# Three pads in SBUF that shift the operand tiles of a long-convolution and MLP kernel

## The chip, the cores and the metric

The kernel runs on one core of a Trainium2 chip. The metric is the device time of one execution in microseconds (us). Three runs of the kernel before are given by their median.

## The reference

Two kinds of layer follow one another twice on a sequence of 2048 tokens with 1024 channels, all in float32. Layer A normalises x, makes a short causal convolution of k (4 taps) times v, convolves that along the sequence with a long filter per channel (through a Fourier transform in the reference), and gates it with the normalised x. Layer B is an MLP with 3584 hidden units and a squared ReLU.

```python
def _A_ref(q, k, v, shift_k, ssm_k, ssm_D):
    ...
    kv = k_shift * v
    ...
    y = y + kv * ssm_D[None, None, :]
    return q * y

def _B_ref(x, w1, b1, w2, b2):
    h = jnp.einsum("bsd,df->bsf", x, w1) + b1
    zero = jnp.zeros_like(h)
    r = jnp.where(h > zero, h, zero)
    h = r * r
    out = jnp.einsum("bsf,fd->bsd", h, w2) + b2
    return out

x = A_q
x = x + _A_ref(_layernorm(x, axis=-1), A_k, A_v, A_shift_k, A_ssm_k, A_ssm_D)
x = x + _B_ref(_layernorm(x, axis=-1), B_w1, B_b1, B_w2, B_b2)
x = x + _A_ref(_layernorm(x, axis=-1), A_k, A_v, A_shift_k, A_ssm_k, A_ssm_D)
x = x + _B_ref(_layernorm(x, axis=-1), B_w1, B_b1, B_w2, B_b2)
```

## The kernel before

The sequence is cut into four blocks of 512 tokens. The long convolution does not depend on the layer's x, so it is made once for each block, and both passes use it. Eight units of MLP work (two passes by four blocks, in the order of ORDER at the top of the file) run one after another on TensorE. The pieces of the convolution of later blocks are slipped between their matmuls by generators (fwd_x and fwd_g from line 352, prod_stream from line 518), paced by a hand-made rate per unit. The first block has a small planner of its own (Plan, first_block, line 1052), which puts its operations in order by estimated costs.

Precision: each float32 operand is split in a high part, rounded to the fast float32 format of TensorE, and a low part, the rest. mm3 (line 333) makes one product as three matmuls, each 128 x 128 stationary by 512 (or 256) moving columns: high by high (line 334), high by low (335), low by high (336). All times of the MLP on TensorE stand on these three lines.

A unit is a list of steps. One step takes one weight tile of 128 x 512 in two parts, whl, and makes 12 matmuls with it:

- "m1" (line 1795): the first product. The stationary operand is a 128-column piece of whl, the moving operand is xh or xl, the two parts of the normalised x of the block, transposed, 8 tiles of 512 columns each.
- "m2" (line 1842): the second product. The stationary operand is a 128-column piece of rh or rl, the two parts of the squared ReLU of the hidden units, and the moving operand is one half of whl (512 columns).
- "w2" (line 1825), in the last three units (WINO): the second product in a scheme with seven products for eight. The stationary operand is a piece of rh and rl, or of sums of these, which relu_w (line 1540) puts into buffers of the convolution that are free by then: high parts in cx and cg, low parts in cp and fy. The moving operand is again a half of whl.

A weight tile comes to whl in one of two ways: as a raw tile wr that ScalarE rounds (line 1006) and VectorE or GpSimd subtracts (line 1014), or, from its second use on, as a stored pair in one load (line 1004). Loads go through SyncE's queue. The matmuls of the convolution on lines 334 to 336 have the constant tables fh, fl, ih, il as stationary operand and fx, fg, yh or yl as moving operand, 256 columns wide. Those of the first block (line 1089) are unsplit float32.

SBUF is given out by pools, one behind another in each partition: const, cv, pre, mw, and then ml. Before ml exists, the pool pro of the first block uses the same place. Inside a pool, the tiles follow one another in the order of their first making. Each is rounded up to a multiple of 32 bytes, and a name with n buffers takes n such places. Every tile starts at the same address in all 128 partitions. All large tiles but fx are multiples of 512 bytes long, so a pool's small tiles and its start decide where the large ones stand modulo 512. In the kernel before this gives:

| tiles | pool | bytes above a multiple of 512 |
|---|---|---|
| ident, fh, fl, ih, il | const | 128 |
| fx (4 buffers of 2080) | cv | 352, 384, 416, 448 |
| yh, yl, fg, cx, cg, cp, fk, sm, fy | cv | 480 |
| px | pre | 448 |
| xh, xl, wr, whl | mw | 384 |
| rh, rl, acc, yt | ml | 0 |

The tile b1t, the biases of the hidden units, is 28 columns of float32 (112 bytes, 128 with rounding) and stands first in ml, ahead of rh. It is loaded once (line 1480) and read by ScalarE (lines 1486 and 1546).

Of the kernel before, what the change touches and what calls it, by code (L numbers as in the profile page):

```python
# [10 lines left out]
F32 = mybir.dt.float32  # L11
# [8 lines left out]
P = 128  # L20
# [4 lines left out]
FT = F // P  # L25
# [22 lines left out]
PACE_SLACK = {1: 74, 3: 10}  # L48
PACE_TO = {1: 2}
PLAIN = 1  # L50
FILL = (16, 45, 8)
WINO = (5, 6, 7)
WMAKE = 4
# [186 lines left out]
def tile_h3_mlp(ctx: ExitStack, tc: tile.TileContext, q, kT, vT, shk, ssmT, ssmD, w1, b1, w2, b2,  # L240
                fwd_t, pro_t, inv_t, sgn_t, out):
    nc = tc.nc
    V, A, G, PE, SY = nc.vector, nc.scalar, nc.gpsimd, nc.tensor, nc.sync
# [3 lines left out]
    const = ctx.enter_context(tc.tile_pool(name="const", bufs=1))  # L247
    cv = ctx.enter_context(tc.tile_pool(name="cv", bufs=1))
    pre = ctx.enter_context(tc.tile_pool(name="pre", bufs=1))
# [13 lines left out]
    def fill(o, n):  # L263
        for _ in range(n):
            PE.transpose(o[:, 0:P], ident, ident)

    def mkfx(shape, dt=F32):
        return cv.tile(shape, dt, name="fx", bufs=4)

    def mkfg(shape, dt=F32):  # L270
        return cv.tile(shape, dt, name="fg", bufs=3)
# [12 lines left out]
    def const_split():  # L284
        if not halved:
            halved.append(True)
            split(plain[0][:, 0:4], fh, fl)
            split(plain[0][:, 4:6], ih, il)
# [5 lines left out]
    epst = const.tile([P, 1], F32)  # L294
    V.memset(epst, EPS)
    warm = const.tile([P, 1], F32)
    A.activation(warm, epst, AF.Copy)

    def tokens(t, b, tt):
# [52 lines left out]
    def fwd_x(sb, c):  # L352
# [18 lines left out]
        yield  # L371
        if sb <= PLAIN:
            xt = mkfx([P, T])
# [11 lines left out]
        for e in range(2):  # L385
            for r in range(2):
                q_ = slice(e * 256, e * 256 + 256)
                ou = oa[e][:, r * 256:r * 256 + 256]
                if sb <= PLAIN:
                    PE.matmul(ou, plain[0][:, 2 * e + r], xt[:, q_], start=True, stop=True)  # L390
# [37 lines left out]
    def fwd_g(sb, c):  # L428
# [7 lines left out]
        for _ in range(FWD_WAIT):  # L436
            yield
        if sb > PLAIN:
            hi = mkfg([P, T], F32R)
# [8 lines left out]
        for r in range(2):  # L448
            ob = oa[r].rearrange("p (b e c) -> p e b c", b=BT, e=2)
            for e in range(2):  # L450
                q_ = slice(e * 256, e * 256 + 256)
                if sb <= PLAIN:
                    PE.matmul(ob[:, e], plain[0][:, 2 * e + r], raw[:, q_], start=True, stop=True)
# [24 lines left out]
        for i in (1, 2, 0):  # L478
# [5 lines left out]
            yield  # L484
        if sb <= PLAIN:
            yield
# [12 lines left out]
    def fwd_stream(kind, fwd):  # L499
        for sb in range(1, NB):  # L500
            if sb > PLAIN:
                const_split()
# [506 lines left out]
    def w_lo():  # L1009
        n = ptr["lo"]  # L1010
        t = wts[n] = his.pop(n)
        if not from_pair(n):
            e = WLO.get(phase[0], "V")
            ENG[e[n % len(e)]].tensor_sub(t[:, 1], raws[n]["t"], t[:, 0].bitcast(F32))  # L1014
            drop(raws.pop(n))
        ptr["lo"] += 1
# [7 lines left out]
    def w_advance(s, w):  # L1024
# [17 lines left out]
        while ptr["lo"] <= w:  # L1042
# [3 lines left out]
                w_hi()  # L1046
            w_lo()

    mw = ctx.enter_context(tc.tile_pool(name="mw", bufs=1))
    rs = {}  # L1050

    def first_block():
# [27 lines left out]
        with tc.tile_pool(name="pro", bufs=1) as pro:  # L1080
# [119 lines left out]
            def carry_part(c, rows, cols):  # L1200
# [3 lines left out]
                def mmk(e):  # L1204
                    if c == KT - 1:
                        fill(o.t, FILL[0])
                    for r in range(2):
# [175 lines left out]
            def tail(t):  # L1383
                x = x1[t]
                norm(ns[t], x, [(x, h) for h in range(KT)], tails[t // 2], t % 2, NORM_0)
                for kh in range(2):
# [3 lines left out]
                    def tr(e, kh=kh, o=o, idle=idle):  # L1390
# [3 lines left out]
                        for x in idle:  # L1394
                            fill(x.t, FILL[2])
                    pl.add([("PE", 600)], tr, [(ns[t], kh)], [o, *idle])
# [79 lines left out]
    xT = first_block()  # L1476
    pds = prod_stream()
    ml = ctx.enter_context(tc.tile_pool(name="ml", bufs=1, reuse_waits="tile"))
    b1t = ml.tile([P, FT], F32, name="b1t", bufs=1)
    SY.dma_start(b1t, b1)  # L1480
    lag = slag

    def relu2(st, k):
# [139 lines left out]
    def chain(accs, b, xh, xl, ready):  # L1623
# [36 lines left out]
        def stage(st, k):  # L1660
# [31 lines left out]
            elif k in (7, 8):  # L1692
                n = k - 7
                for kh in range(2):
                    o = ps1()
                    if tts[n] == 2 and kh == 0:
                        fill(o, FILL[1])
                    for c in range(4):
# [267 lines left out]
```

## Time and profile before

| what | value |
|---|---|
| runs of the kernel before | 2758.86, 2754.60, 2755.72 us |
| median | 2755.72 us |
| the profiled execution, from its first to its last instruction | 2756.1 us |
| mean granted TensorE clock | 0.992 |
| matmuls, as many weight loads | 12601 |
| data moved by DMA | 756.88 MB, 275 GB/s in the mean |

The profiled execution is as long as its span of 2756.1 us; nothing around it is listed apart. PE is TensorE's matmuls, PEld its weight loads, DVE VectorE, ACT ScalarE, POOL GpSimd, SP SyncE. In a group line, `out<-in` are the names of the tiles written and read, `x` the count, then busy time in us, mean of one in ns, and the idle time of the engine just before, with what ended it. Matmuls overlap one another: the time from one start to the next start is shorter than the duration of one. In a line of the timeline the first number is the start in us, the second the duration. In a line of the view by windows there follow, behind the window and its length, the busy time and count of each engine (all of them, or the chosen one), the granted clock, the DMA share and GB/s. In a line of the waits: who waited for whom, us in total, times, and the longest.

### The profile page before, as it was taken

What the parts mean: (1) busy time and instruction counts of PE and PEld (TensorE: products, weight loads), DVE (VectorE), ACT (ScalarE), POOL (GpSimd) and SP (SyncE); (2) the same over time, 40 slices, a digit from 0 to 9 for tenths busy, and PEclk for the clock granted to TensorE, in tenths of its full rate; (3) what the DMA queues carried; (4) which work ended last, traced back from release to release, by engine and by line L of the source; (5) the groups of instructions that cost most, each with busy time, mean ns of one, the idle gap of its engine ahead of it and who ended that gap; (6) DMA issues with size and microseconds to landing.
All of it is one profiled execution on the core that took longest, in us unless ns stands there. A gap on an engine that the chain in (4) does not pass through costs nothing.

```text
span 2756.1 us, 36563 instructions
## 1 busy us (share of the span) xinstructions
PE 2694.2 (98%) x12601; PEld 2237.7 (81%) x12601; DVE 1935.9 (70%) x3068; ACT 1110.9 (40%) x1937; POOL 826.3 (30%) x531
## 2 busy tenths in 40 slices
PE   7999899899999999999999999999999999999999
PEld 7888787887788888888788888888788788888887
DVE  7878797677787677778676655376787666664555
ACT  4354344433434333342233422244355454444443
POOL 2345564244542645326454265000100010001000
PEclk9999999999999999999999999999999999999999
DMA  8889898589988898788887877688898766676555
GB/s 260 267 298 321 281 311 287 199 302 351 305 294 308 305 330 294 272 303 302 317 286 259 310 270 286 217 290 292 303 308 274 289 229 214 226 275 204 176 164 202
DMA packets 378057, 756.88 MB, mean 275 GB/s; under 512 B 43904, under 2 KB 159248, under 8 KB 377872
## 3 DMA queue, kind: packets, MB, share of 16 engines
q1 hardware_dynamic: 377872, 754.55, 79.8%
q8 instruction: 99, 1.62, 0.2%
q14 instruction: 86, 0.70, 0.1%
HBM read 604.46 MB, written 149.95 MB: 274 GB/s over the span
## 4 chain that ended last, share of the span: by engine, by line
PE 86%; DVE 6%; DMA 5%; issue 1%; ACT 1%; SPq 1%; POOL 0%; DVEq 0%; ACTq 0%; POOLq 0%
PE p L334 26%; PE p L335 26%; PE p L336 26%; PE p L1089 2%; DMA wr<-w 1%; PE pt L336 1%; PE pt L335 1%; PE pt L334 1%; DVE whl L1014 1%; DMA whl<-wd_m 1%; DMA wd_m<-whl 0%; PE pt L594 0%; PE p L788 0%; DVE sm L528 0%; DMA cg<-gd 0%
## 5 line engine op out<-in xcount | busy, mean ns | idle before, releaser
L334 PE MATMUL p<-xh,whl 128*128 128x512 f32 (+1 forms) x1840 | 710.3, 386 | 20.2 <-DVE rl L1492 19.0
L524 POOL TENSOR_TENSOR cp<-cx,cg 128x384 f32<-128x384 f32 (+5 forms) x288 | 534.0, 1867 | 617.7 <-DVE sm L528 397.7
L336 PE MATMUL p<-xh,whl 128*128 128x512 f32 (+1 forms) x1840 | 705.9, 384 | 0.0
L335 PE MATMUL p<-xl,whl 128*128 128x512 f32 (+1 forms) x1840 | 705.5, 383 | 0.1
L1006 ACT CAST whl<-wr 128x512 fp32r<-128x512 f32 x638 | 385.9, 622 | 450.1 <-PE p L336 274.8
L334 PE MATMUL p<-whl,rh 128*128 128x512 f32 x1372 | 547.8, 399 | 1.8 <-DMA whl<-wd_m 1.7
L335 PE MATMUL p<-whl,rh 128*128 128x512 f32 x1372 | 543.0, 396 | 4.9 <-DVE whl L1014 4.9
L1014 DVE TENSOR_TENSOR whl<-wr,whl 128x512 fp32r<-128x512 f32 x624 | 489.4, 805 | 76.9 <-ACT whl L1006 72.1
L336 PE MATMUL p<-whl,rl 128*128 128x512 f32 x1372 | 542.3, 395 | 0.0
L334 PEld LDWEIGHTS p<-xh,whl 128*128 128x128 f32 x1840 | 347.7, 189 | 91.0 <-DVE rl L1492 11.9
L336 PEld LDWEIGHTS p<-xh,whl 128*128 128x128 f32 x1840 | 347.4, 189 | 68.2
L335 PEld LDWEIGHTS p<-xl,whl 128*128 128x128 f32 x1840 | 347.6, 189 | 66.5 <-DVE xl L1402 0.3
L335 PEld LDWEIGHTS p<-whl,rh 128*128 128x128 f32 x1372 | 259.4, 189 | 64.0 <-DVE whl L1014 6.4
L334 PEld LDWEIGHTS p<-whl,rh 128*128 128x128 f32 x1372 | 259.2, 189 | 62.2 <-DMA whl<-wd_m 4.0
L336 PEld LDWEIGHTS p<-whl,rl 128*128 128x128 f32 x1372 | 259.0, 189 | 60.7
L528 DVE TENSOR_REDUCE sm<-cp 128x128 f32<-128x384 f32 (+5 forms) x288 | 249.8, 875 | 13.2 <-POOL cp L524 11.4
L1590 POOL TENSOR_TENSOR acc<-acc,px 128x512 f32<-128x512 f32 x18 | 23.1, 1318 | 770.3 <-DMA px<-b 770.3
L1486 ACT ACTIVATE p<-p,b1t 128x512 f32<-128x512 f32 x138 | 91.7, 664 | 395.6 <-PE p L336 395.4
L1492 DVE TENSOR_TENSOR rl<-p,rh 128x512 fp32r<-128x512 f32 x138 | 94.9, 688 | 221.0 <-ACT rh L1489 220.8
L1554 DVE TENSOR_TENSOR rl<-wr,rh 128x256 fp32r<-128x256 f32 x84 | 51.0, 607 | 207.6 <-ACT rh L1549 207.4
L1613 DVE TENSOR_TENSOR acc<-p,acc 128x512 f32<-128x512 f32 x152 | 101.5, 688 | 90.8 <-PE p L336 90.3
L1546 ACT ACTIVATE wr<-p,b1t 128x512 f32<-128x512 f32 x84 | 58.0, 690 | 188.5 <-PE p L336 184.9
(280 smaller groups left out, 3306.0 us busy)
## 6 DMA issues: line engine op xcount, KB each, us to landing
whl<-wd_m SPq DMA_DIRECT2D x382, 512.0 KB, 5.1
wr<-w SPq DMA_DIRECT2D x494, 256.0 KB, 5.3
wr<-td SPq DMA_DIRECT2D x152, 256.0 KB, 4.2
wd_m<-whl SPq DMA_DIRECT2D x70, 512.0 KB, 6.2
cx<-xd SPq DMA_DIRECT2D x48, 512.0 KB, 5.4
cg<-gd SPq DMA_DIRECT2D x48, 512.0 KB, 6.5
gd<-fg SPq DMA_DIRECT2D x72, 256.0 KB, 6.7
cx<-xd SPq DMA_DIRECT2D x48, 384.0 KB, 6.1
```

Source lines behind the costliest of these rows:

```text
L334: PE.matmul(o, lh, rh, start=start, stop=False)
L335: PE.matmul(o, lh, rl, start=False, stop=False)
L336: PE.matmul(o, ll, rh, start=False, stop=stop)
L524: G.tensor_mul(pr.rearrange("p c i -> p i c"), xt[:, 0:j + 1], gt[:, j::-1])
L528: V.tensor_reduce(sm[:, ty, jj], st["pr"], axis=AX.X, op=OP.add)
L1006: A.copy(t[:, 0], raws[n]["t"])
L1014: ENG[e[n % len(e)]].tensor_sub(t[:, 1], raws[n]["t"], t[:, 0].bitcast(F32))
L1089: PE.matmul(o, lh, r, start=start, stop=stop)
L1486: A.activation(o, o, AF.Relu, bias=b1t[:, st["f"]:st["f"] + 1])
L1492: V.tensor_sub(st["lo"], o, st["hi"].bitcast(F32))
L1546: A.activation(r, st["o"], AF.Relu, bias=b1t[:, st["f"]:st["f"] + 1])
L1613: V.tensor_add(accs[tt][:, d], o, accs[tt][:, d])
```

## The change

Two tiles that nobody reads are added, and one tile is widened.

- pad_c, 104 columns of float32 (416 bytes), at the end of the pool const. It moves everything behind it.
- pad_p, 24 columns (96 bytes), the first tile of the pool pre. Each of the two pads is set to 0 once by VectorE.
- b1t, from 28 to 128 columns (512 bytes), the first tile of the pool ml. Its load writes the first 28 columns as before.

```diff
+PAD_C, PAD_P = 104, 24
...
     warm = const.tile([P, 1], F32)
+    pad_c = const.tile([P, PAD_C], F32)
+    V.memset(pad_c, 0.0)
     A.activation(warm, epst, AF.Copy)
...
+    pad_p = pre.tile([P, PAD_P], F32)
+    V.memset(pad_p, 0.0)
     mw = ctx.enter_context(tc.tile_pool(name="mw", bufs=1))
...
-    b1t = ml.tile([P, FT], F32, name="b1t", bufs=1)
-    SY.dma_start(b1t, b1)
+    b1t = ml.tile([P, P], F32, name="b1t", bufs=1)
+    SY.dma_start(b1t[:, 0:FT], b1)
```

Adding the bytes to the table above (416 for cv, 416 + 96 = 512 for the large tiles of pre and for mw, and 512 + 512 - 128 for rh, rl, acc and yt) gives, modulo 512: fx 256, 288, 320, 352; yh, yl, fg, cx, cg, cp, fk, sm and fy 384; px 448; xh, xl, wr and whl 384; rh, rl, acc and yt 384. The tables of the pool const stay at 128. No instruction of the MLP or of the convolution is added, removed or moved in its order.

## The prediction

> **What bounds the kernel now.** I began with the page of the profile, for the span, the busy shares and the chain of waits that ended last.
>
> ```profile
> span 2756.1 us, 36563 instructions
> PE 2694.2 (98%) x12601; PEld 2237.7 (81%) x12601; DVE 1935.9 (70%) x3068; ACT 1110.9 (40%) x1937; POOL 826.3 (30%) x531
> ...
> PE 86%; DVE 6%; DMA 5%; issue 1%; ACT 1%; SPq 1%; POOL 0%; DVEq 0%; ACTq 0%; POOLq 0%
> ```
>
> The second line and the third say the same thing in two ways: TensorE is busy for 98% of the span, and 86% of the last chain is matmuls behind matmuls. So the time is, to first order, the number of matmuls times the step from one matmul to the next. A change that only moves addresses can matter here in one way: by changing that step. The next view is the groups by line with shapes kept apart, restricted to TensorE.
>
> ```profile
> L334 PE MATMUL p<-xh,whl 128*128 128x512 f32 x1712 | 673.6, 393 | 20.2 <-DVE rl L1492 19.0 <-DMA whl<-wd_m 1.2
> ...
> L334 PE MATMUL p<-whl,rh 128*128 128x512 f32 x1372 | 547.8, 399 | 1.8 <-DMA whl<-wd_m 1.7
> L335 PE MATMUL p<-whl,rh 128*128 128x512 f32 x1372 | 543.0, 396 | 4.9 <-DVE whl L1014 4.9
> L336 PE MATMUL p<-whl,rl 128*128 128x512 f32 x1372 | 542.3, 395 | 0.0
> L336 PE MATMUL p<-whl,cp 128*128 128x512 f32 x264 | 104.6, 396 | 0.0
> L334 PE MATMUL p<-whl,cg 128*128 128x512 f32 x168 | 67.0, 399 | 1.3 <-DMA whl<-wd_t 1.3
> L334 PE MATMUL p<-whl,cx 128*128 128x512 f32 x168 | 66.8, 397 | 0.0
> L335 PE MATMUL p<-whl,cg 128*128 128x512 f32 x168 | 66.7, 397 | 0.3 <-DVE whl L1014 0.3
> L335 PE MATMUL p<-whl,cx 128*128 128x512 f32 x168 | 66.6, 396 | 0.0
> ...
> L336 PE MATMUL p<-whl,fy 128*128 128x512 f32 x72 | 28.5, 396 | 0.0
> ```
>
> Three families of 512-column matmuls carry the kernel. In the first (first product, three lines of x1712) the stationary operand is a piece of whl and xh or xl moves. In the second (3 x 1372 = 4116) the stationary operand is a piece of rh or rl and whl moves. In the third (264 + 4 x 168 + 72 = 1008) it is a piece of cx, cg, cp or fy, and again whl moves. The mean of one, 393 to 399 ns, is longer than the step, because matmuls overlap. The step has to be read from starts. I looked in the timeline for long stretches of one family without a stop and took the first and last start of each.
>
> ```profile
> 1427.58 0.40 PE L334 MATMUL p<-whl,rh 128*128 128x512 f32 x1
> 1427.82 0.40 PE L335 MATMUL p<-whl,rh 128*128 128x512 f32 x1
> 1428.06 0.39 PE L336 MATMUL p<-whl,rl 128*128 128x512 f32 x1
> ...
> 1446.87 0.39 PE L336 MATMUL p<-whl,rl 128*128 128x512 f32 x1
> ```
>
> ```profile
> 2054.59 0.39 PE L334 MATMUL p<-whl,cx 128*128 128x512 f32 x1
> ...
> 2076.84 0.39 PE L336 MATMUL p<-whl,cp 128*128 128x512 f32 x1
> ```
>
> ```profile
> 2077.07 0.39 PE L334 MATMUL p<-xh,whl 128*128 128x512 f32 x1
> ...
> 2120.36 0.40 PE L336 MATMUL p<-xh,whl 128*128 128x512 f32 x1
> ```
>
> The view by windows gives the counts and what else ran.
>
> ```profile
> 1427.60:1446.90 19.30, 19.30 (x85) 15.65 (x84) 18.55 (x21) 6.02 (x12) 13.41 (x7) 1.00 0.87 307
> 2054.60:2076.95 22.35, 22.35 (x97) 17.99 (x96) 17.28 (x32) 8.20 (x14) 0.00 (x0) 1.00 0.85 284
> 2077.10:2120.50 43.40, 43.40 (x193) 35.95 (x192) 32.24 (x68) 21.14 (x35) 0.00 (x0) 1.00 0.92 305
> ```
>
> Each window holds one more matmul than its stretch, the one before it, still running. So 84, 96 and 192 starts: (1446.87 - 1427.58) / 83 = 232.4 ns, (2076.84 - 2054.59) / 95 = 234.2 ns, (2120.36 - 2077.07) / 191 = 226.65 ns. The column before last but one is the granted clock, 1.00 in all three. All are 128x128 by 512 in the same number format, and all run in the same rhythm of high, high, low part. The DMA share is the next column: it is highest (0.92) in the fastest stretch, so traffic is not what slows the others.
>
> What does sort them is the address. Taken modulo 512 bytes, by the allocation told above: first product, stationary 384 and moving 384; second product, stationary 0 and moving 384; third family, stationary 480 and moving 384. Equal gives 226.65, a difference of 128 gives 232.4, one of 96 gives 234.2.
>
> **The change part by part.** The second pad and the first together leave mw where it was modulo 512, at 384: the first product keeps its 226.65 ns. The first pad brings cx, cg, cp, fy, yh, yl and fg from 480 to 384, and the widened b1t brings rh and rl from 0 to 384. So both slower families come to equal offsets, the state that this trace shows in the first product, and I take its step for them.
>
> Second product: 4116 x (232.4 - 226.65) = 23.7 us. Third family: 1008 x (234.2 - 226.65) = 7.6 us. Together 31.3 us, against a span of 2756.1 us that lies 0.4 us over the median of the runs, 2755.7.
>
> The Trainium skill speaks against this. "SBUF — State Buffer", section "SBUF: two separate sides", has TensorE on ports of its own that never wait for anybody, and "TensorE: Matmul & The Clock Gate", section "Back-to-back issue gap", makes the gap a function of the column count alone. By these pages the sum would be 0. The three steps at one column count, one clock and one shape, 7.6 ns apart, do not agree with them.
>
> How much of the 31.3 us reaches the end depends on whether TensorE's suppliers follow. The same view by windows, first for all of TensorE and then for the tile rl, which takes one matmul in three of the second product:
>
> ```profile
> 135.00:1000.00 865.00, 833.33 (x4050) 0.98 0.88 299
> 1000.00:2756.10 1756.10, 1745.50 (x7812) 1.00 0.76 264
> ...
> 135.00:1000.00 865.00, 199.77 (x504) 0.98 0.88 299
> 1000.00:2756.10 1756.10, 342.49 (x868) 1.00 0.76 264
> ```
>
> After 1000 us TensorE is idle for 10.6 of 1756 us: it sets the pace, and a shorter step is a shorter stretch. That part holds 868 of 1372, or 15.0 us of the second product, and, as the stretch at 2054 shows, the third family with its 7.6: 22.6 us. Between 135 and 1000 us TensorE stands idle for 31.7 of 865 us, and 8.7 us of the gain lie there. The waits name who is late:
>
> ```profile
> PE p L334 <- DVE rl L1492: 19.0, 6, 5.0
> ...
> PE pt L419 <- DVE fx L366: 6.1, 1, 6.1
> PE p L335 <- DVE whl L1014: 5.2, 2, 4.9
> ```
>
> ```profile
> SPq L1004 <- PE p L336: 737.6, 282, 12.3
> ```
>
> Where TensorE waits, it waits for VectorE, which does not become faster. If VectorE's own queue sets the distance between two such stops, TensorE only arrives there earlier and waits longer. I have no row that divides these 8.7 us; the ends are none and all of it lost, and I take half, 4.4, because TensorE still works 96% of that stretch. The last row is why I charge nothing for the loads: 282 times the queue that fetches weights waited for a matmul to release a buffer, 737.6 us in all, so weights arrive early and follow a faster TensorE. The forecast gain is 31.3 - 4.4 = 26.9 us.
>
> The other matmuls have operands whose relation changes without becoming equal, since fh, fl, ih and il stay at 128 while yh, yl and fg move. They are 256 columns wide, twelve groups:
>
> ```profile
> L336 PE MATMUL pt<-fg,fl 128*128 128x256 f32 x64 | 18.1, 283 | 0.0
> ...
> L336 PE MATMUL pt<-yh,il 128*128 128x256 f32 x32 | 9.3, 291 | 0.0
> ```
>
> Six groups of 64 and six of 32 make 576. No row shows them at the new offsets. The spread between best and worst relation at 512 columns is 7.6 ns; for half the columns I bound it by half, 3.8 ns either way, so 2.2 us either way, and take 0. The shares of the last chain by line give the matmuls of the first block:
>
> ```profile
> PE p L334 26%; PE p L335 26%; PE p L336 26%; PE p L1089 2%; DMA wr<-w 1%; PE pt L336 1%; PE pt L335 1%; PE pt L334 1%; DVE whl L1014 1%; DMA whl<-wd_m 1%; DMA wd_m<-whl 0%; PE pt L594 0%; PE p L788 0%; DVE sm L528 0%; DMA cg<-gd 0%
> ```
>
> These unsplit matmuls (L1089) have 2% of it, 55 us. With the same spread, 7.6 / 226.65 = 3.4%, that is 1.8 us either way, again taken as 0.
>
> What the change adds is two memsets on VectorE. The start of the timeline shows one like them and the hole they fall into:
>
> ```profile
> 0.81 0.06 DVE L295 MEMSET epst<- 128x1 f32 x1 [0.81 <-PEq L1958]
> ...
> 5.65 0.28 DVE L1434 TENSOR_TENSOR xh<-xh 8x128 f32<-8x128 f32 x1 [4.78 <-DMA xh<-ssmD]
> ```
>
> For 104 and 24 columns I bound each between 0.06 and 0.28 us, the second row being an operation on 128 columns. VectorE is idle for 4.78 us there, waiting for a load, so they are hidden; without that cover they would cost at most 0.56 us. Nobody reads the pads, so nothing waits for them. The load of b1t keeps its bytes and its place in the queue.
>
> **The rivals.** *No change:* the step depends on the role, not on the address. Each family has its own operands, and no stretch shows the second product at equal offsets, so the trace cannot exclude that a moving whl, or a stationary operand freshly written, costs 6 to 8 ns by itself. Time 2755.7. Against it: the second and third family have the same moving operand and kind of stationary operand, and still differ by 1.8 ns. The two pages of the Trainium skill that I cited would have it so.
>
> *Slower:* equal offsets are the bad case and the first product escapes it. In its stretch the next weight load and the matmul start together:
>
> ```profile
> 2080.70 0.39 PE L335 MATMUL p<-xl,whl 128*128 128x512 f32 x1
> 2080.70 0.19 PEld L336 LDWEIGHTS p<-xh,whl 128*128 128x128 f32 x1
> ```
>
> With equal offsets both streams then begin at the same place modulo 512. If that collides, and the second product with its freshly written tiles meets it on each matmul, its step would rise to the worst that the rows show, 0.24 us (1427.58 to 1427.82 to 1428.06): 4116 x 7.6 ns + 1008 x 5.8 ns = 37 us more, 2793 us. It decides as soon as the new step is over 232.4. Against it: the first product has just this coincidence and is the fastest.
>
> **How the numbers follow.** Forecast, both families at the step of the first product: chance 0.85. No change: 0.10. Slower: 0.05. The time is 2755.7 - 26.9 = 2728.8, say 2729 us. Within the forecast the gain lies between 22.6 - 2.2 - 1.8 = 18.6 us (all that precedes 1000 us lost) and 31.3 + 4.0 = 35.3 us, so 2720 to 2737 us. The runs before spread over 4.3 us, which I add on both sides: 2716 to 2741. That leaves out both rivals, 0.15, and about 0.05 of the forecast's own. Over 0.2% (5.5 us, about what a measurement of this kernel can tell from no change) faster has 0.85, within it 0.10, slower 0.05.
>
> **What would show it.** In the changed profile the stretches of the second product and third family should step by 226 to 227 ns, with the first product unmoved; TensorE's count and the granted clock stay; the idle time of TensorE before 1000 us grows by some 4 us, with the same releasers, and after 1000 us does not. The prediction is wrong if either family keeps its 232 or 234 ns, or if the steps shorten and the idle time grows by as much.

## The result and the profile after

The changed kernel takes 2733.70 us in the median of 4 runs (2727.79 to 2737.36), the kernel before 2757.29 us in the median of 4 (2754.60 to 2761.55; one run more than above). The ratio is 0.9907, with a 95% interval of 0.9888 to 0.9925: 20.7 to 30.9 us faster, 25.6 in the middle. The medians themselves are 23.6 us apart. The profiled execution, which took 2727.79 us, spans 2726.0 us, 30.1 us less than the span before; it is the fastest of the four.

The page of the changed kernel, the lines that answer to those of before (three lines of code have been added above mm3, so its matmuls now stand on lines 337 to 339):

```profile
span 2726.0 us, 36565 instructions
PE 2666.4 (98%) x12601; PEld 2235.5 (82%) x12601; DVE 1933.7 (71%) x3070; ACT 1108.8 (41%) x1937; POOL 826.1 (30%) x531
...
PE 82%; DVE 8%; DMA 6%; issue 1%; ACT 1%; POOL 1%; SPq 1%; DVEq 0%; POOLq 0%; ACTq 0%
```

The same 12601 matmuls keep TensorE busy 27.8 us less. VectorE has two instructions more, the memsets. The last chain goes through matmuls for 82% instead of 86%: suppliers end a little more of it.

The groups by line with shapes kept apart, one of each family (busy us, mean ns of one):

```profile
L337 PE MATMUL p<-xh,whl 128*128 128x512 f32 x1712 | 672.5, 393 | 18.8 <-DVE rl L1497 15.1 <-DVE acc L1602 1.5 <-DMA whl<-wd_m 1.4
...
L338 PE MATMUL p<-whl,rh 128*128 128x512 f32 x1372 | 536.2, 391 | 4.4 <-DVE whl L1017 4.2
...
L338 PE MATMUL p<-whl,cx 128*128 128x512 f32 x168 | 65.4, 389 | 0.0
```

The first product keeps its 393 ns; the second product goes from 396 to 391, the third family from 396 to 389. The step itself is again read from first and last starts of long stretches in the timeline: 95 matmuls of the second product, 96 of the third family, 192 of the first product.

```profile
458.04 0.39 PE L337 MATMUL p<-whl,rh 128*128 128x512 f32 x1
...
479.35 0.39 PE L338 MATMUL p<-whl,rh 128*128 128x512 f32 x1
...
2031.75 0.39 PE L337 MATMUL p<-whl,cx 128*128 128x512 f32 x1
...
2053.28 0.39 PE L339 MATMUL p<-whl,cp 128*128 128x512 f32 x1
2053.51 0.39 PE L337 MATMUL p<-xh,whl 128*128 128x512 f32 x1
...
2096.80 0.39 PE L339 MATMUL p<-xh,whl 128*128 128x512 f32 x1
```

They give 21.31 / 94 = 226.7 ns, 21.53 / 95 = 226.6 ns and 43.29 / 191 = 226.65 ns. The two slower families have come to the step of the first. The rhythm has changed too: in these stretches every start follows the one before by 226 or 227 ns, while in the stretch of the second product before, at 1427 us, single starts lay 228 to 241 ns apart. The 232.4 ns there are a mean.

### The profile page after: what moved, and what is told of

It is laid out like the page before. It is cut to its first block, busy times and chain, and to the rows that moved or that the text cites. A ratio compares the mean times of both kernels' runs of the same rounds, so it can differ in the third digit from the quotient of the medians.

```text
span 2726.0 us, 36565 instructions
## 1 busy us (share of the span) xinstructions
PE 2666.4 (98%) x12601; PEld 2235.5 (82%) x12601; DVE 1933.7 (71%) x3070; ACT 1108.8 (41%) x1937; POOL 826.1 (30%) x531
## 4 chain that ended last, share of the span: by engine, by line
PE 82%; DVE 8%; DMA 6%; issue 1%; ACT 1%; POOL 1%; SPq 1%; DVEq 0%; POOLq 0%; ACTq 0%
PE p L337 25%; PE p L338 25%; PE p L339 25%; PE p L1094 2%; DMA wr<-w 2%; DVE whl L1017 1%; DMA whl<-wd_m 1%; PE pt L339 1%; PE pt L337 1%; PE pt L338 1%; DMA cg<-gd 1%; DVE sm L531 1%; DVE fx L367 0%; PE pt L422 0%; PE pt L597 0%
## 5 line engine op out<-in xcount | busy, mean ns | idle before, releaser
L1017 DVE TENSOR_TENSOR whl<-wr,whl 128x512 fp32r<-128x512 f32 x624 | 496.8, 816 | 74.3 <-ACT whl L1009 71.6
L337 PE MATMUL p<-whl,rh 128*128 128x512 f32 x1372 | 540.9, 394 | 2.8 <-DMA whl<-wd_m 2.4
L338 PE MATMUL p<-whl,rh 128*128 128x512 f32 x1372 | 536.2, 391 | 4.4 <-DVE whl L1017 4.2
L339 PE MATMUL p<-whl,rl 128*128 128x512 f32 x1372 | 535.7, 390 | 0.0
```

Source lines behind the costliest of these rows:

```text
L337: PE.matmul(o, lh, rh, start=start, stop=False)
L338: PE.matmul(o, lh, rl, start=False, stop=False)
L339: PE.matmul(o, ll, rh, start=False, stop=stop)
```

## Where the time went

All kernels here but those of the last two experiments (half_stationary and half_at_128) run the same matmuls in the same order, so one matmul can be followed. The one that started at 135.0 us before starts at 135.9 now, and the one that started at 1000.1 starts at 988.9. The view by windows, TensorE alone, from the first mark to the second and from there to the end: the kernel before, the changed kernel, and a third kernel with the same three steps that is told below (common_416):

```profile
135.00:1000.10 865.10, 833.42 (x4051) 0.98 0.88 299
1000.10:2756.10 1756.00, 1745.40 (x7812) 1.00 0.76 264
```

```profile
135.90:988.90 853.00, 824.57 (x4051) 0.98 0.89 303
988.90:2726.00 1737.10, 1723.43 (x7812) 1.00 0.78 267
```

```profile
136.00:994.90 858.90, 826.20 (x4050) 0.98 0.88 301
994.90:2730.90 1736.00, 1722.57 (x7812) 1.00 0.77 267
```

Length less busy time is idle time. Between the marks, the changed kernel gains 12.1 us, and TensorE is idle for 28.4 us instead of 31.7. After the second mark, it gains 18.9 us, and idle time grows from 10.6 to 13.7 us. Ahead of the first mark it loses 0.9 us, which makes the 30.1 in all. The third kernel gains 6.2 us between the marks and 20.0 after them. The shorter step is the same in both executions; the waits between the marks differ by 4.3 us.

A small part of these gains is the clock and not the step. Each execution has a few short stretches in which TensorE is granted half its clock (0.50 in the third column from the end), here two of those of the kernel before and one of the changed kernel:

```profile
294.70:301.50 6.80, 3.01 (x9) 0.50 0.68 225
1318.70:1322.10 3.40, 3.40 (x12) 0.50 1.04 349
```

```profile
41.20:44.60 3.40, 3.40 (x13) 0.50 0.96 265
```

Between the marks such stretches add up to 37.5 us before and 34.1 us in the changed kernel, and the one at 1318 us has no counterpart in the changed kernel, while the one at 41 us has none before. Counting half of such a stretch as lost, an estimate, the clock gave the changed kernel 1.7 us between the marks and 1.7 us after them, and took 1.7 us ahead of the first.

The waits name the same releasers as before:

```profile
PE p L337 <- DVE rl L1497: 15.1, 5, 5.1
...
PE pt L422 <- DVE fx L369: 5.9, 1, 5.9
PE p L338 <- DVE whl L1017: 4.8, 2, 4.2
```

## Experiments

The theory: the step is set by the distance from the moving to the stationary tile in SBUF, modulo some power of two. The rivals: a place modulo 512 that is good in itself; a number that belongs to the family of matmuls; something else that the pads moved.

**Each part alone**, and the whole once more, all on one chip.

```diff
 only_b1t: the two pads are taken out
-PAD_C, PAD_P = 104, 24
...
-    pad_c = const.tile([P, PAD_C], F32)
-    V.memset(pad_c, 0.0)
...
-    pad_p = pre.tile([P, PAD_P], F32)
-    V.memset(pad_p, 0.0)
 only_pads: b1t is as before
-    b1t = ml.tile([P, P], F32, name="b1t", bufs=1)
+    b1t = ml.tile([P, FT], F32, name="b1t", bufs=1)
```

> Only b1t is widened, so rh and rl stand at 384 modulo 512 and the third family stays at 480. If the distance of the stationary from the moving tile sets the step, the second product steps by 226.7 ns and the third family keeps 234.2: a profiled span about 22 us under the 2756.1 of before. If the pads moved something else that matters, the second product keeps 232.4 ns and the span stays within 3 us of before.

> Only the two pads, so the third family (cx, cg, cp, fy) comes to 384 and rh, rl stay at 0. By the distance theory the third family steps by 226.7 ns, the second product keeps 232.4, and the span is about 7 us shorter than before. If the step hangs on rh and rl alone, the third family keeps 234.2 ns and nothing is gained.

> The changed kernel once more, beside its two parts on one chip. The sum of the parts' gains by the distance theory, about 22 and 7 us, should be its gain: 26 to 31 us under before. If half of what lies ahead of 1000 us is lost to waits on VectorE, it is 26; if none of it, 30.

| kernel | median us | ratio to before, 95% | gain us | span us | second product ns | third family ns |
|---|---|---|---|---|---|---|
| before | 2757.40 | | | 2756.1 | 232.4 | 234.2 |
| only_b1t | 2736.74 | 0.9920 (0.9905 to 0.9935) | 22.1 | 2735.4 | 226.7 | 234.3 |
| only_pads | 2753.51 | 0.9978 (0.9966 to 0.9990) | 6.1 | 2753.2 | 232.4 | 226.8 |
| after_again | 2734.14 | 0.9901 (0.9885 to 0.9917) | 27.3 | 2725.3 | 226.7 | 226.7 |

(Gain: the distance of the ratio from 1, times 2757.4.) The timeline of only_b1t, first and last start of 95 and of 96 matmuls:

```profile
457.09 0.39 PE L334 MATMUL p<-whl,rh 128*128 128x512 f32 x1
...
478.40 0.39 PE L335 MATMUL p<-whl,rh 128*128 128x512 f32 x1
...
2035.64 0.39 PE L334 MATMUL p<-whl,cx 128*128 128x512 f32 x1
...
2057.90 0.39 PE L336 MATMUL p<-whl,cp 128*128 128x512 f32 x1
```

and of only_pads:

```profile
460.05 0.40 PE L337 MATMUL p<-whl,rh 128*128 128x512 f32 x1
...
481.90 0.39 PE L338 MATMUL p<-whl,rh 128*128 128x512 f32 x1
...
2057.45 0.39 PE L337 MATMUL p<-whl,cx 128*128 128x512 f32 x1
...
2079.00 0.39 PE L339 MATMUL p<-whl,cp 128*128 128x512 f32 x1
```

Each part moves the step of its own family and leaves the other's: 226.7 beside 234.3, and 232.4 beside 226.8. The gains by the ratios, 22.1 and 6.1 us, have the expected 22 and 7 within their intervals, and add up to 28.2 beside 27.3 for the whole. (The medians themselves are 20.7, 3.9 and 23.3 us apart, and the profiled span of only_pads is shorter by 2.9 us and not by 7: a few us are within what executions differ by.) With the steps, this settles that the gain comes from these two families. The repeated kernel does not choose between 26 and 30: its interval, 23 to 32 us, holds both.

**Another common place.** All tiles of the three families at 416 in place of 384.

```diff
-PAD_C, PAD_P = 104, 24
+PAD_C, PAD_P = 112, 24
```

> Eight more columns in the first pad: all tiles of the three families stand together at 416 modulo 512 in place of 384, still equal to one another. If only the distance counts, all three families step by 226.7 ns. If 384 itself is the good place, a multiple of 128, all three become slower, by up to the 5.7 to 7.6 ns that the other places cost before: 30 us or more over the changed kernel, since the first product would lose too.

It took 2732.65 us, span 2730.9. 95 starts of the second product (458.05 to 479.36) step by 226.7 ns, 96 of the third family (2330.24 to 2351.77) by 226.6, 192 of the first product (1976.97 to 2020.26) by 226.65. So 384 is not a place that is good in itself.

**The first product made unequal.** Weights moved against x; the second product stays equal, at 0.

```diff
-        big = {nm: new(mw, nm, 1, [P, KT * T]) for nm in ("xh", "xl")}
+        big = {nm: new(mw, nm, 1, [P, KT * T + 32 * (nm == "xl")]) for nm in ("xh", "xl")}
```

> xl is made 32 columns (128 bytes) longer, so whl stands at 0 modulo 512, rh and rl at 0 too, xh and xl at 384, cx, cg, cp and fy at 384. Now the first product has its stationary tile 128 bytes ahead of the moving one, as the second product had in the kernel before, and the second product is equal at 0. By the distance theory the first product steps by 232.4 ns (5100 matmuls by 5.7 ns, about 29 us longer than the changed kernel), the second by 226.7 ns; the third family has a distance of 384, for which there is no row yet. If the step hangs on the role or on 384 itself, the first product keeps 226.7 and the second goes back to 232.4.

It took 2764.80 us, span 2763.0. First and last start of 192 matmuls of the first product:

```profile
2077.54 0.39 PE L337 MATMUL p<-xh,whl 128*128 128x512 f32 x1
...
2121.92 0.39 PE L339 MATMUL p<-xh,whl 128*128 128x512 f32 x1
```

44.38 / 191 = 232.4 ns. The family that had always been the fastest takes the step that the second product had at the same distance of 128. The third family, now at 384, steps by 232.4 too (96 starts, 2055.22 to 2077.30). TensorE is busy for 2701.3 us, 34.9 more than in the changed kernel: some 29 for the first product, as expected, and 5.8 for the third family (1008 x 5.8 ns). The time itself shows less. The one execution of the kernel before on that chip took 2751.54 us, 13.3 less, where the steps would give some 4; but executions of the kernel before on one chip lay up to 11 us apart (2754.45 to 2765.20). So the number does not belong to the family.

**Other distances.** The widths of the pads and of b1t set the distance of the third family and of the second product, with whl left at 384.

```diff
 d256_d128
-PAD_C, PAD_P = 104, 24
+PAD_C, PAD_P = 8, 120
-    b1t = ml.tile([P, P], F32, name="b1t", bufs=1)
+    b1t = ml.tile([P, 64], F32, name="b1t", bufs=1)
 d96_d256:  40, 88 and 152
 d64_d32:   112, 16 and 144
 d160_d192: 24, 104 and 40
```

> Distances of the stationary tile ahead of the moving one: 256 bytes in the second product, 128 in the third family. By the distance theory the third family at 128 steps as the second product did at 128, 232.4 ns, and not 234.2 as it did at 96. For 256 there is no row; if any unequal distance costs alike, 232 to 234 ns. If the family sets its own number, the third family shows another step than 232.4.

> Distances: 96 bytes in the second product, 256 in the third family. By the distance theory the second product now steps by 234.2 ns as the third family did at 96, and the third family by what the second product shows at 256. If the family matters, the second product at 96 is not at 234.2.

> Distances: 64 bytes in the second product, 32 in the third family, both smaller than any seen so far. If the cost grows as the distance gets smaller (96 costs 7.6 ns, 128 costs 5.7), both step by more than 234.2 ns; if it falls to zero smoothly towards equality, they lie between 226.7 and 234.2. A step under 226.7 would mean that equality is not the best place.

> Distances of the stationary tile ahead of the moving one: 160 bytes in the second product, 192 in the third family. The runs so far have 226.7 ns at 0 and 256, 233.3 at 32 and 64, 234.2 at 96 and 232.4 at 128 and 384, which repeats every 256 bytes. If every distance but a multiple of 256 costs, both lie between 230 and 236 ns. If some distance beats equality, one of them is under 226.7.

A last one sets a distance under the 32 bytes to which tiles are rounded: xh and xl are used from their fifth column on, so they begin at 400, and 8 more columns of xl move whl to 416.

```diff
-        xh = mw.tile([P, KT, T], F32R, name="xh", bufs=1)
-        xl = mw.tile([P, KT, T], F32R, name="xl", bufs=1)
+        xh = mkx3("xh")
+        xl = mkx3("xl")
... (four more places in the same way)
+    def mkx(nm, dt=F32R):
+        return mw.tile([P, KT * T + (128 if nm == "xh" else 8)], dt, name=nm, bufs=1)[:, 4:4 + KT * T]
+
+    def mkx3(nm):
+        return mkx(nm).rearrange("p (k t) -> p k t", k=KT)
```

> xh and xl are used from 16 bytes into their places, whl stands at 416 modulo 512, so the first product has a distance of 16 bytes, the smallest yet, the second product 0, the third family 480 (224 modulo 256). If any inequality of the addresses costs, the first product steps by about 233 ns, as at 32 bytes. If the cost comes in with the size of the distance, it lies between 226.7 and 233.

The timelines, first and last start of 95 matmuls of the second product or 96 of the third family: d256_d128, distances 256 and 128,

```profile
460.45 0.39 PE L337 MATMUL p<-whl,rh 128*128 128x512 f32 x1
...
481.76 0.39 PE L338 MATMUL p<-whl,rh 128*128 128x512 f32 x1
...
2339.37 0.40 PE L337 MATMUL p<-whl,cx 128*128 128x512 f32 x1
...
2361.45 0.40 PE L339 MATMUL p<-whl,cp 128*128 128x512 f32 x1
```

d160_d192, third family at 192,

```profile
2055.40 0.40 PE L337 MATMUL p<-whl,cx 128*128 128x512 f32 x1
...
2077.16 0.39 PE L339 MATMUL p<-whl,cp 128*128 128x512 f32 x1
```

and x_off16, 192 matmuls of the first product at 16:

```profile
2077.43 0.40 PE L337 MATMUL p<-xh,whl 128*128 128x512 f32 x1
...
2121.99 0.40 PE L339 MATMUL p<-xh,whl 128*128 128x512 f32 x1
```

They give 226.7, 232.4, 229.0 (229.05 by these rounded starts) and 233.3 ns. Single executions took 2747.32 us (d256_d128), 2758.71 (d96_d256) and 2761.24 (d64_d32), beside 2751.54 of the kernel before on the same chip, and 2755.98 (d160_d192) and 2765.83 (x_off16), beside 2759.75 on theirs. One execution each is too few to set times against each other here; the steps carry the argument. All distances that were run, each from such a stretch:

| stationary ahead of moving, bytes | step ns | seen in |
|---|---|---|
| 0 | 226.7 | all three families |
| 16 | 233.3; in other stretches 236.5 | first product, x_off16 |
| 32 | 233.4 | third family, d64_d32 |
| 64 | 233.3 | second product, d64_d32 |
| 96 | 234.2, 234.3 | third family, before; second product, d96_d256 |
| 128 | 232.4 in all three; in other stretches of the first product 233.3 | second product, before; third family, d256_d128; first product, whl_apart |
| 160 | 233.3 | second product, d160_d192 |
| 192 | 229.0 | third family, d160_d192 |
| 256 | 226.7 | second product, d256_d128; third family, d96_d256 |
| 384 | 232.4 | third family, whl_apart |
| 480 | 233.4 | third family, x_off16 |

In these stretches the same distance gives the same step whatever the family. 256 is as good as 0 and 384 as bad as 128, which fits a pattern that repeats every 256 bytes; a multiple of 256 would have done. The repeat rests on 256 above all, since 384 is also 128 the other way round modulo 512. Being off by 16 bytes costs at least as much as being off by 64. No distance tried is faster than equality. Three guesses fell: that the cost grows towards small distances, that it fades smoothly, and that every distance but a multiple of 256 costs 230 ns or more (192 has 229.0).

The distance does not fix the step alone. In x_off16 the first product has 28 stretches of at least 60 starts at full clock without a stop: 17 step by 233.3 ns, and 11 by 236.3 to 236.7, with starts 234 and 239 ns apart by turns. One of these, 132 starts in 30.98 us, 236.5 ns:

```profile
963.87 0.39 PE L337 MATMUL p<-xh,whl 128*128 128x512 f32 x1
...
994.85 0.39 PE L339 MATMUL p<-xh,whl 128*128 128x512 f32 x1
```

In whl_apart, at 128, 21 such stretches step by 232.3 to 232.4 ns and 7 by 233.3. Tiles, shape and clock are the same in both kinds; what chooses between them is not shown. At equal offsets there is no second kind: all stretches of the changed kernel lie between 226.7 and 227.1 ns.

**Half a stationary tile**, to find what the equal step itself is made of. These two kernels leave out half of the output rows of the steps concerned.

```diff
-                mm3(os[tt], r["hi"][:, t], r["lo"][:, t], wh, wl, i == 0, i == FC - 1)
+                n = P if i in (0, FC - 1) else P // 2
+                h = slice(tt * P, tt * P + n)
+                mm3(os[tt][0:n], r["hi"][:, h], r["lo"][:, h], wh, wl, i == 0, i == FC - 1)
 half_at_128, further:
-    b1t = ml.tile([P, P], F32, name="b1t", bufs=1)
+    b1t = ml.tile([P, FT], F32, name="b1t", bufs=1)
```

> In the second product of units 0 to 4, the stationary operand has 64 columns in place of 128 in five of seven steps; it leaves out half of those steps' output rows. Distances are equal. The equal step is 226.7 ns for 512 columns and 120.0 for 256, so 106.7 per 256 columns and 13.3 ns on top in both. If these 13.3 ns are the reading of the stationary tile (512 bytes a partition) out of the moving operand's time, half a tile costs 6.7: a step of 220.0 ns. If they are a fixed cost of an instruction, 226.7 stays.

> The same with rh and rl at a distance of 128 bytes, where the full stationary tile steps by 232.4 ns; it leaves out the same rows. If the cost of distance, 5.7 ns, belongs to the reading of the stationary tile, half a tile pays about half: 220.0 + 2.9 = 222.9 ns. If it belongs to the moving operand or to the instruction, it stays at 5.7 ns over the step of the equal one.

They took 2741.62 and 2749.18 us. First and last start of 60 such matmuls, half_stationary and then half_at_128:

```profile
1029.15 0.40 PE L337 MATMUL p<-whl,rh 128*64 128x512 f32 x1
...
1042.72 0.39 PE L339 MATMUL p<-whl,rl 128*64 128x512 f32 x1
```

```profile
1033.28 0.39 PE L337 MATMUL p<-whl,rh 128*64 128x512 f32 x1
...
1046.81 0.39 PE L339 MATMUL p<-whl,rl 128*64 128x512 f32 x1
```

13.57 / 59 = 230.0 ns and 13.53 / 59 = 229.3 ns. Both expectations fail. Half the stationary data at equal offsets is slower than the whole, 230.0 beside 226.7, and with 64 columns equality has no advantage any more: a distance of 128 is faster by some 0.6 ns, in each of the eleven unbroken stretches of 60 that either kernel has (229.3 to 229.4 beside 229.9 to 230.0). So the 13.3 ns of the expectation are not a charge that grows with the stationary bytes. That the step hangs on how the two streams of reads fall against each other in time would fit this, and the two steps at a distance of 16; it is argued, not shown. What happens in the memory at that moment is not shown by any of these runs, and stays open.

## Why the prediction was right, step by step

*TensorE sets the pace, and a change of addresses can matter through the step only.* Right: the spans differ by 30.1 us, of which 27.8 are TensorE's busy time; some 1.7 us of the 30.1 are the clock's, by the estimate above.

*The step is sorted by the address, and both slower families take 226.65 ns.* Right in both profiled executions of the changed kernel, and shown by the parts alone, by whl_apart and by the table of distances. The rival without change and the slower one both fall here: the same role at another distance has another step, and equality at 384, 416 or 0 is the fastest place. Written as a matter of 512 bytes, the reason was too strict, since 256 does as well. And the address alone is not the whole of it: at 16 and at 128 the first product has two steps each.

*31.3 us, of which 26.9 arrive.* The size was right: 25.6 us (20.7 to 30.9) in the first comparison, 27.3 (22.9 to 31.7) in the second. The time came out 4.9 us over the forecast 2728.8: the median of the kernel before rose by 1.6 us with its fourth run, and the medians are 23.6 us apart. (The span of before was set beside that median as if the two were one measure. The recorded times are 1.8 us longer than their spans, 2727.79 beside 2726.0, so that execution lay some 2 us over the median and not 0.4; the gain does not hang on it.)

The two pages of the Trainium skill that were weighed against it, "SBUF — State Buffer" (section "SBUF: two separate sides") and "TensorE: Matmul & The Clock Gate" (section "Back-to-back issue gap"), have no rule by which the place of a tile would change TensorE's step, so the sum by them would be 0. On this point the runs disagree with them: at one column count and a granted clock of 1.00, the step goes from 226.7 to 234.3 ns where only addresses were changed.

*Half of the 8.7 us ahead of 1000 us is lost, nothing after it.* Here the split was off, though the sum came out near. The profiled execution lost nothing ahead of the mark (12.1 us gained, 3.3 of it shorter waits and some 1.7 the clock), and common_416 gained 6.2 there. After the mark, 18.9 and 20.0 us arrived of the 22.6, and idle time grew by 3.1 and 2.8 us. Both signs that were named for the idle time failed: ahead of the mark it was to grow by some 4 us and changed by -3.3 and +1.0, after it it was to stay. So the waits took some of the gain after the mark, and those ahead of it vary by several us between executions of one set of steps. The two errors have opposite signs, and that the sum of 26.9 came out as near as it did is in part luck. The runs of the changed kernel lie up to 9.6 us apart; the longer ones were not profiled, so how much of that is waits and how much clock stays open.

*The other matmuls cost nothing on balance; the memsets are hidden.* Over all starts at full clock without a stop between them, the split matmuls of the convolution step by 118.7 ns before and 118.9 now, and the 256-column ones of the first block by 216.1 in both: within the bounds. The pads' memsets and the first operation after them, in the timeline of the changed kernel:

```profile
0.86 0.14 DVE L299 MEMSET pad_c<- 128x104 f32 x1
0.96 0.08 DVE L1053 MEMSET pad_p<- 128x24 f32 x1
5.20 0.28 DVE L1439 TENSOR_TENSOR xh<-xh 8x128 f32<-8x128 f32 x1 [4.17 <-DMA xh<-ssmD]
```

They take 0.14 and 0.08 us, and 4.17 us of waiting for a load still follow. The queue that fetches weights still waits for matmuls, so the loads followed:

```profile
SPq L1007 <- PE p L339: 715.4, 280, 12.6
```

## What to carry to other kernels

Where TensorE runs back to back, read the step from start to start, for each family of matmuls, and compare families of one shape: a mean duration or a busy share shows little of a difference of 3%. If they differ, look at where their stationary and moving tiles begin in SBUF; here, for full tiles and 512 moving columns, bringing the starts to equal places was worth 5.7 ns of 232.4 and 7.6 ns of 234.2 per matmul, and cost under a thousand bytes a partition. Try the distance on the chip for other widths, since the good one did not carry over to 64 stationary columns or, as told next, to 256 moving ones.

## What was not expected of the hardware

A distance of 256 bytes is as good as none, 16 bytes off are at least as bad as 64 off, and one distance can have two steps. For 256 moving columns the order turns round: in the first product's half blocks, 154 starts at equal offsets step by 18.35 / 153 = 119.9 ns in the changed kernel, and at a distance of 16 bytes (x_off16) by 17.92 / 153 = 117.1 ns:

```profile
532.94 0.28 PE L338 MATMUL pt<-xl,whl 128*128 128x256 f32 x1
...
551.29 0.28 PE L338 MATMUL p<-xl,whl 128*128 128x256 f32 x1
```

```profile
535.24 0.28 PE L338 MATMUL pt<-xl,whl 128*128 128x256 f32 x1
...
553.16 0.28 PE L338 MATMUL p<-xl,whl 128*128 128x256 f32 x1
```

At a distance of 128 (whl_apart), two such stretches step by 118.6 and 118.7 ns and a third by 119.9. Equal offsets are thus the best of those tried for 512 columns, and for 256 no better than either of the other two. Only 480 matmuls of the first product are that narrow, so at 2.8 ns each this kernel would gain little, 1.3 us, from it.
